# Cross-covariance attention into a folded MLP: block 2 of the fold ahead of the first tile, and w_in's first 512 columns loaded ahead of v

## The chip, the cores and the metric

The kernel runs on one core of a Trainium2 chip. The core has five engines with a queue each: TensorE (PE; its weight loads are shown as PEld), VectorE (DVE), ScalarE (ACT), GpSimd (POOL) and SyncE (SP). Sixteen DMA engines move data between memory and the on-chip buffer SBUF. PE writes its results to PSUM, which is divided into banks of 2 KB per partition. The metric is the time of one execution on the device in microseconds (us). A profile is one execution, with every instruction's start and duration; its times count from the first instruction.

## The reference

There are four batches of 6080 tokens, and 256 channels.

```python
qn = q / (np.linalg.norm(q, axis=1, keepdims=True) + 1e-06)   # norms over the 6080 tokens
kn = k / (np.linalg.norm(k, axis=1, keepdims=True) + 1e-06)
s = kn.transpose(0, 2, 1) @ qn / tau                          # 256 x 256 in each batch
a = softmax(s)                                                # over the last axis
x = (v @ a).reshape(24320, 256)
h = x @ w_in                                                  # w_in: 256 x 2048
g = s_moe * maximum(h, 0) ** 2 + b_moe
out = g @ w_out                                               # w_out: 2048 x 256
```

`tau` is 1.0. All inputs and the output are float32; the kernel works in float16 with float32 sums.

## The kernel before, in words

Attention and the first layer are folded into one matrix. With e the unnormalised exponentials, v @ a @ w_in = v @ (a @ w_in), and wa = a @ w_in is a 256 x 2048 matrix for each batch. So there is one product v @ wa for each tile of 512 tokens, then relu, the square, and the product with w_out. There are 48 tiles (the last is half a tile), and each takes 16 steps, one per slice of 128 hidden columns. `mm1(g, m)` (L744) makes slice m of tile g on PE: two products (one for each half of the 256 channels) of a 128x128 piece of `wa` with `vT`, the transposed tile of v. ACT then takes the relu of two slices at a time (L771), the squares are shared by DVE and ACT, and the second product follows later (L932, or L836 for the plain first tile).

Before the first tile, batch 0 has a prologue of its own. q and k are loaded in chunks through POOL's DMA queue, and cast to float16 on the way. PE sums the Gram matrix `s_ps` (L154). The norms come from squares, summed with ones on PE (`n_ps`, L252 and L256), and four ACT steps (L277) make their inverses. `scale` (L302, DVE) and `exps` (L308, ACT) make the exponentials `eT`, in two halves j = 0, 1. Batches 1 to 3 do the same later, spread out between the steps of the tiles.

Nothing reorders these instructions: `po` keeps every engine's instructions in the order in which the program is written. Semaphores between engines, and the choice of PSUM banks and buffers, are worked out when the kernel is built, from what each instruction reads and writes.

What touches the change:

- *Loads* (L524 to L539). POOL's queue gets, in this order: v's first tile, w_in's columns 0 to 255, 256 to 511, 512 to 1023, 1024 to 1535, 1536 to 2047, v's second tile, and four pieces of w_out. At most eight loads are under way; a load is issued when the one eight places before has landed.
- *The transposes* (`transpose_v(0)`, L594 and L463). Eight PE products with an identity turn v's first tile into `vT_ps`, one PSUM bank in float16. DVE copies it to `vT` in one instruction of 128x1024 (L471).
- *One idle matmul* (`keep_busy(1)`, L595 and L554). It has no use but to keep PE active.
- *The first block* (`first_block(2 * P)`, L340). For each half j of `eT`: two products for the row sums `r_ps` (L347), and two products with w_in's columns 0 to 255 (L352), for the two halves m of wa's rows. These lie in two banks. DVE takes the reciprocal of the sums (L356). Then `scaled` (L325) multiplies 128 columns at a time by it, into `wa`: m = 0 on ACT (L329), m = 1 on DVE (L331).
- *The other blocks* (`fold_one`, L361, listed at L430). Columns 256 to 511 (block 2), 512 to 767, 768 to 1023, 1024 to 1535 and 1536 to 2047, each in two halves m: two products each (L336) and a `scaled`. `FOLDS` (L667) puts them behind `mm1` of steps 0, 0, 1, 1, 3, 3, 5, 5, 8, 8 of the first tile. PE's order before is thus: transposes, idle matmul, first block, `mm1(0, 0)`, block 2, `mm1(0, 1)`, block at 512, `mm1(0, 2)`, and so on.
- *Banks.* Batch 0 takes its fold results from three banks in turn (`ps_o`, by `bank`, L442), `r_ps` among them. `s_ps` has a bank of its own.

Of the kernel before, what the change touches and what calls it, by code (L numbers as in the profile page):

```python
# [9 lines left out]
FP32 = mybir.dt.float32  # L10
# [6 lines left out]
def kernel(  # L17
# [12 lines left out]
    nc = tc.nc  # L30
    P = 128

    B, N, C = q.shape
# [11 lines left out]
    CH = C // P  # L45
# [9 lines left out]
    def po(ins):  # L55

        tc.keep_in_program_order(ins)
        return ins

    def pool(name, bufs, **kw):  # L60
        return ctx.enter_context(tc.tile_pool(name=name, bufs=bufs, **kw))
# [19 lines left out]
    ps_gram = pool("ps_gram", 1, space=PSUM)  # L81
# [4 lines left out]
    w_in16 = wpool.tile([P, CH, Dff], FP16)  # L86
# [4 lines left out]
    def h_tile(name):  # L91
        return ps_h.tile([P, 2, TG], FP32, tag="h_ps", name=name)
# [19 lines left out]
    class Gram:  # L112
# [147 lines left out]
        def finish_ops(self):  # L260

            st = {}

            def inverse(a=None):

                n = C + CH if a is None else (CH, C)[a]

                def part(i):
                    if i == 0:
                        st["r", a] = sm_pool.tile([P, n], FP32, tag=f"r{a}", name=f"r{a}")  # L270
                        if a is None:
                            st["r", 1], st["r", 0] = st["r", a][:, :C], st["r", a][:, C:]
                    r = st["r", a]
                    func, kw = [(AF.Ln, dict(bias=tiny)), (AF.Exp, dict(scale=0.5)),
                                (AF.Ln, dict(bias=eps)), (AF.Exp, dict(scale=-1.0))][i]
                    sums = self.n_all if a is None else self.n_ps[a]
                    po(nc.scalar.activation(out=r, in_=r if i else sums, func=func, **kw))  # L277
                    if i == 3 and a != 1 and inv_tau != 1.0:
                        po(nc.vector.tensor_scalar_mul(
                            out=st["r", 0], in0=st["r", 0], scalar1=inv_tau))  # L280

                return [lambda i=i: part(i) for i in range(4)]

            def norms(a):
                return lambda: self.add_norms(a, last=True)
# [9 lines left out]
            def scale(halves=1):  # L295
                rk, src = st["r", 1], st.get("t", self.s_ps)
                if "t" not in st:
                    st["t"] = sm_pool.tile([P, CH, C], FP32, tag="sm_t", name="sm_t")
                for h in range(halves):
                    js = slice(h, h + 1) if halves == CH else slice(0, CH)  # L300
                    n = js.stop - js.start
                    po(nc.vector.tensor_mul(st["t"][:, js], src[:, js],  # L302
                                            rk[:, None, :].broadcast_to((P, n, C))))

            def exps(j):
                if j == 0:
                    st["e"] = sm_pool.tile([P, CH, C], FP16, tag="eT", name="eT")
                po(nc.scalar.activation(  # L308
                    out=st["e"][:, j, :], in_=st["t"][:, j], func=AF.Exp,
                    scale=st["r", 0][:, j : j + 1]))  # L310
                if j == 0:
                    self.wa = apool.tile([P, CH, Dff], FP16, tag="wa16", name="wa16")
# [11 lines left out]

            def scaled(f0, n, m, wa_ps):  # L325
                dst = self.wa[:, m, ds(f0, n)]
                third = self.b == 0 and f0 == 2 * NW
                if m == third and not (self.b == 0 and NW <= f0 < 2 * NW):
                    po(nc.scalar.mul(out=dst, in_=wa_ps, mul=st["rs"][:, m : m + 1]))  # L329
                else:  # L330
                    po(nc.vector.tensor_scalar_mul(  # L331
                        out=dst, in0=wa_ps, scalar1=st["rs"][:, m : m + 1]))
# [4 lines left out]
                                        w_in16[:, j, ds(f0, n)],  # L337
                                        start=(j == 0), stop=(j == CH - 1)))

            def first_block(n):  # L340

                two = [self.bank("wa_ps", CH, C)[:, 0, :n], h_tile("wa_ps")[:, 0, :n]]
                r_ps = self.bank("r_ps", CH, C)[:, :, 0]
                for j in range(CH):
                    exps(j)
                    for ch in range(CH):
                        po(nc.tensor.matmul(r_ps[:, ch : ch + 1], st["e"][:, j, ts(ch, P)],  # L347
                                            parts16, start=(ch == 0 and j == 0),
                                            stop=(ch == CH - 1 and j == CH - 1),
                                            skip_group_check=True))  # L350
                    for m in range(CH):
                        po(nc.tensor.matmul(two[m], st["e"][:, j, ts(m, P)],  # L352
                                            w_in16[:, j, :n],
                                            start=(j == 0), stop=(j == CH - 1)))
                st["rs"] = sm_pool.tile([P, CH], FP32, tag="rs", name="rs")
                po(nc.vector.reciprocal(out=st["rs"], in_=r_ps))  # L356
                for f0 in range(0, n, P):
                    for m in range(CH):
                        scaled(f0, P, m, two[m][:, ds(f0, P)])

            def fold_one(f0, n, m):  # L361
                def f():
                    wa_ps = self.bank("wa_ps", CH, C).rearrange("p a c -> p (a c)")[:, :n]
                    fold_mm(f0, n, m, wa_ps)
                    if self.b == 0 and f0 == 2 * NW and m == 1:
                        return at_step(5, lambda: scaled(f0, n, m, wa_ps))
                    scaled(f0, n, m, wa_ps)
                return f
# [58 lines left out]
                ]  # L427

            if self.b == 0:
                blocks = [(2 * P, 2 * P), (4 * P, 2 * P), (6 * P, 2 * P), (2 * NW, NW), (3 * NW, NW)]  # L430
                folds = [fold_one(f0, n, m) for f0, n in blocks for m in range(CH)]
                return [norms(1), *inverse(1), norms(0), *inverse(0), lambda: scale(CH),
                        lambda: first_block(2 * P)] + folds

            def sums_and_halves():
                sums()
# [12 lines left out]
    def group(g):  # L449
        t0 = g * TG  # L450
        return t0, min(TG, NT - t0) // P

    v_tiles, vT_tiles = {}, {}

    def load_v(g):
        t0, nj = group(g)
        v16 = vpool.tile([P, TG // P, C], FP16, tag="v16", name="v16")
        po(nc.gpsimd.dma_start(  # L458
            out=v16[:, :nj, :],
            in_=v_flat[t0 : t0 + nj * P, :].rearrange("(p j) c -> p j c", j=nj)))  # L460
        v_tiles[g] = v16

    def transpose_v(g):  # L463
        _, nj = group(g)
        v16 = v_tiles.pop(g)
        vT_ps = ps_o.tile([P, CH, TG], FP16, tag="o_ps", name="vT_ps")
        for j in range(nj):
            for ch in range(CH):
                po(nc.tensor.transpose(vT_ps[:, ch, ts(j, P)], v16[:, j, ts(ch, P)], ident16))  # L469
        vT = vtpool.tile([P, CH, TG], FP16, tag="vT", name="vT")  # L470
        po(nc.vector.tensor_copy(out=vT[:, :, : nj * P], in_=vT_ps[:, :, : nj * P]))  # L471
        vT_tiles[g] = vT

    def crossbar_v(g):

# [31 lines left out]
    for c in range(NDIRECT, len(g0.chunks) - NLATE):  # L507
        g0.load(c)
        if c == NDIRECT:
            po(nc.gpsimd.affine_select(  # L510
                out=ident16, in_=ones_id, compare_op=ALU.is_equal, fill=0.0, base=0,
# [5 lines left out]
    NW = 512  # L517
    w_in_rows = moe_w_in.rearrange("(co p) f -> p co f", p=P)

    def load_w_in(f0, f1, co=None):  # L520
        cs = slice(0, CH) if co is None else slice(co, co + 1)
        po(nc.gpsimd.dma_start(out=w_in16[:, cs, f0:f1], in_=w_in_rows[:, cs, f0:f1]))

    load_v(0)  # L524
    load_w_in(0, 2 * P)
    load_w_in(2 * P, NW)
    load_w_in(NW, 2 * NW)
    load_w_in(2 * NW, 3 * NW)
    load_w_in(3 * NW, Dff)
# [21 lines left out]
    def keep_busy(n):  # L551

        for _ in range(n):
            po(nc.tensor.matmul(h_tile("idle_ps")[:, 0, :], fill[:, :P], fill, start=True,  # L554
                                stop=True, skip_group_check=True))

    norms_k, *rest = g0.finish_ops()
    inverse_k, norms_q, inverse_q, scale_s, first_block, folds = (
        rest[:4], rest[4], rest[5:9], rest[9], rest[10], rest[11:])
# [31 lines left out]
            g0.add_norms(0)  # L591
    for f in (*inverse_q, scale_s):
        f()
    transpose_v(0)  # L594
    keep_busy(1)  # L595
    first_block()


    acc = opool.tile([P, 4, C], FP32, tag="o_sb", name="acc")
# [64 lines left out]
    FIN = (0, 3, 5, 7, 9, 11, 13, 17, 19, 22,  # L664
           25, 27, 31, 33, 35, 37, 39, 41, 43, 47, 49, 51, 53, 55)
    first_group = [b * N // TG for b in range(B)]
    FOLDS = (0, 0, 1, 1, 3, 3, 5, 5, 8, 8)  # L667
    for i, f in enumerate(folds):
        early.setdefault(FOLDS[i], []).append(f)
    at_step(14, lambda: po(nc.vector.tensor_scalar_mul(  # L670
        out=s_out, in0=s_bc, scalar1=1.0 / (LAM * LAM))))
# [29 lines left out]
    for b in range(1, B):  # L701
# [6 lines left out]
        n = NCH * JC  # L708
# [247 lines left out]
    for s in range(NS + FT):  # L956
        g, m = divmod(s, FT)
# [8 lines left out]
        if work:  # L966
            items, n = work[0]
# [61 lines left out]
```

## Time and profile before

| What | us |
|---|---|
| median of 3 runs | 714.37 (714.33 to 714.67) |
| profiled execution: span, first to last instruction | 712.9 |
| profiled execution: its total | not on its page; the runs' median lies 1.5 above the span |
| PE busy, share of the span | 692.9 (97%) |
| DVE busy | 635.6 (89%) |
| ACT busy | 547.5 (77%) |
| first product of the first tile (L761) starts | 37.84 |
| PE idle just ahead of it | 0.48 |

In the lines shown below, a row of the chain has a start, a length, an engine and its work; a row of the timeline has a start, the time that the group took, the engine, line, operation, output and inputs, count and, in brackets, how long the engine was idle before and what ended that. In the table of stretches each engine has busy us and a count of instructions, followed by the granted TensorE clock (1.00 is full speed), the DMA engines' share and GB/s. The lines of the queues have packets, MB and the share of sixteen engines. The granted clock is the share of full speed at which PE was let run.

### The profile page before, as it was taken

How to read it: one execution, taken by the hardware profiler on the slowest of the kernel's cores; microseconds unless marked ns; L12 is line 12 of the kernel's file. 1: busy time of each engine (PE TensorE's matmuls, PEld its weight loads, DVE VectorE, ACT ScalarE, POOL GpSimd, SP SyncE). 2: the span in 40 equal slices, each digit the busy share in tenths (PEclk: the TensorE clock that was granted, in tenths of full speed). 3: DMA queues.
4: the chain of work that ended last, by engine and by line, in shares of the span. 5: the costliest groups of instructions: out<-in, count | busy, mean ns of one | idle time of the engine just before them, and what ended most of it. 6: DMA issues, size and time to landing. Idle time of an engine off the chain costs nothing.

```text
span 712.9 us, 17531 instructions
## 1 busy us (share of the span) xinstructions
PE 692.9 (97%) x7422; PEld 502.9 (71%) x7422; DVE 635.6 (89%) x906; ACT 547.5 (77%) x598; POOL 114.1 (16%) x192
## 2 busy tenths in 40 slices
PE   3699999999999999999999999999999999999998
PEld 2456777776677777777677777777768777777777
DVE  4889999999988989998999899998998888888886
ACT  5689877787777777778877777777876777777875
POOL 4533132201202222111010222111000000000000
PEclk9999999999999999999999999999999999999999
DMA  9999999566566878465761888737323333321202
GB/s 213 207 259 168 186 164 137 114 109 122 105 136 109 133 137 144 110 92 101 156 131 50 148 134 150 129 76 96 101 65 75 94 71 75 97 61 46 83 31 75
DMA packets 87854, 83.55 MB, mean 117 GB/s; under 512 B 56368, under 2 KB 62784, under 8 KB 87776
## 3 DMA queue, kind: packets, MB, share of 16 engines
q0 software_dynamic: 27136, 44.00, 38.9%
q1 hardware_dynamic: 60128, 37.45, 21.1%
q8 instruction: 58, 0.95, 0.6%
q10 hardware_dynamic: 512, 0.98, 0.4%
q14 instruction: 20, 0.16, 0.1%
HBM read 78.91 MB, written 24.90 MB: 146 GB/s over the span
## 4 chain that ended last, share of the span: by engine, by line
PE 95%; DMA 4%; ACT 1%; issue 0%; DVE 0%; ACTq 0%; POOLq 0%
PE h_ps L761 46%; PE o_ps L932 40%; PE s_ps L154 5%; DMA qk<-in_q_dram 2%; DMA qk<-in_k_dram 1%; PE wa_ps L394 1%; PE o_ps L836 1%; PE o_ps L808 0%; PE wa_ps L336 0%; ACT r L277 0%; PE n_ps L252 0%; ACT sq L185 0%; ACT eT L308 0%; PE vT_ps L469 0%; DVE half L229 0%
## 5 line engine op out<-in xcount | busy, mean ns | idle before, releaser
L771 ACT ACTIVATE r<-h_ps 128x1024 f16<-128x1024 f32 (+1 forms) x384 | 388.5, 1013 | 144.2 <-PE h_ps L761 140.6
L761 PE MATMUL h_ps<-vT,wa 128*128 128x512 f16 (+7 forms) x1632 | 452.1, 364 | 0.5 <-ACT wa L329 0.5
L932 PEld LDWEIGHTS <-S 128*128 128x128 f16 x2944 | 198.1, 98 | 84.3
L932 PEld LDWEIGHTS <-g 128*128 128x128 f16 x2208 | 155.0, 98 | 74.0
L784 DVE TENSOR_TENSOR g<-r 128x2048 f16<-128x2048 f16 (+2 forms) x150 | 174.4, 1163 | 10.1 <-ACT r L771 9.7
L932 PE MATMUL o_ps<-T,S 128*128 128x128 f16 x2208 | 183.1, 219 | 0.0
L761 PEld LDWEIGHTS <-wa 128*128 128x128 f16 x1632 | 136.6, 98 | 19.0 <-ACT wa L329 1.0
L932 PE MATMUL o_ps<-w_out,g 128*128 128x128 f16 x1472 | 134.2, 219 | 0.0
L782 ACT ACTIVATE g<-r 128x1024 f16<-128x1024 f16 (+1 forms) x97 | 100.3, 1034 | 0.2
L789 DVE SCALAR_TENSOR_TENSOR o_sb<-o_ps,s_out,u 128x256 f32<-128x256 f32 x138 | 66.2, 480 | 36.1 <-PE o_ps L932 34.5
L154 PE MATMUL s_ps<-qk 128*128 128x256 f16 (+1 forms) x384 | 71.0, 287 | 15.6 <-ACT qk L145 11.0
L458 POOL DMA_DIRECT2D v<-in_v_dram x48 | 31.4, 662 | 239.9 <-DMA vT<-v 192.7
L215 POOL DMA_DIRECT2D f<-f x33 | 28.8, 874 | 245.9 <-DVE f L199 197.3
L789 DVE SCALAR_TENSOR_TENSOR u<-o_ps,s_out,rowconst 128x256 f32<-128x256 f32 x138 | 65.7, 476 | 0.0
L932 PE MATMUL o_ps<-w_out,S 128*128 128x128 f16 x736 | 63.5, 219 | 0.0
L932 PE MATMUL o_ps<-N,g 128*128 128x128 f16 x736 | 63.4, 219 | 0.0
L185 ACT ACTIVATE sq<-qk 128x1024 f16<-128x1024 f16 (+2 forms) x53 | 54.5, 1041 | 4.5 <-DMA qk<-in_k_dram 1.9
L861 DVE TENSOR_TENSOR S<-S,g 128x2048 f16<-128x2048 f16 (+1 forms) x47 | 56.4, 1200 | 1.2
L859 DVE TENSOR_TENSOR S<-g 128x2048 f16<-128x2048 f16 (+1 forms) x47 | 56.0, 1192 | 0.0
L863 DVE TENSOR_TENSOR S<-g 128x2048 f16<-128x2048 f16 x46 | 55.8, 1214 | 0.0
L865 DVE TENSOR_TENSOR S<-g,S 128x2048 f16<-128x2048 f16 x46 | 55.8, 1213 | 0.0
L154 PEld LDWEIGHTS <-qk 128*128 128x128 f16 (+1 forms) x384 | 33.0, 103 | 21.2 <-ACT qk L145 11.0
(103 smaller groups left out, 334.4 us busy)
## 6 DMA issues: line engine op xcount, KB each, us to landing
out_dram<-o_sb SPq DMA_DIRECT2D x43, 512.0 KB, 3.0
v<-in_v_dram POOLq DMA_DIRECT2D x47, 256.0 KB, 5.0
qk<-in_q_dram POOLq DMA_DIRECT2D x43, 256.0 KB, 7.7
qk<-in_k_dram POOLq DMA_DIRECT2D x42, 256.0 KB, 6.4
f<-f POOLq DMA_DIRECT2D x30, 128.0 KB, 3.1
vT<-v SPq DMA_TRANSPOSE x182, 3.0
w<-in_moe_w_out_dram POOLq DMA_DIRECT2D x4, 512.0 KB, 9.9
out_dram<-o_sb SPq DMA_DIRECT2D x8, 256.0 KB, 4.1
```

Of the source, the lines that this page charges most:

```text
L154: po(nc.tensor.matmul(self.s_ps[:, ch, :], qc[:np_, j, ts(ch, P)], kc[:np_, j, :], start=(c == 0 and j == 0 and ch == 0), stop=(c == len(s ...
L185: po(nc.scalar.activation(out=st["sq"][:np_, a, js, :], in_=(qc, kc)[a][:np_, js, :], func=AF.Square))
L761: po(nc.tensor.matmul(dst, wa[:, ci, ts(m, P)], src, start=(ci == 0), stop=(ci == CH - 1), skip_group_check=True))
L771: po(nc.scalar.activation(out=r16[:, :, i % 2, :n], in_=h_tiles.pop((g, i))[:, :, :n], func=AF.Relu))
L782: po(nc.scalar.activation(out=dst, in_=src, func=AF.Square))
L784: po(nc.vector.tensor_mul(dst, src, src))
L789: po(nc.vector.scalar_tensor_tensor(out=dst, in0=src, scalar=s_out, op0=ALU.mult, in1=add, op1=ALU.add))
L859: po(nc.vector.tensor_add(T[1], A21, A22))
L861: po(nc.vector.tensor_sub(T[2], T[1], A11))
L863: po(nc.vector.tensor_sub(T[3], A11, A21))
L865: po(nc.vector.tensor_sub(T[4], A12, T[2]))
L932: po(nc.tensor.matmul(st[name][:, j, :], a()[:, i, ts(j, P)], w[:, i, :], start=first, stop=last, skip_group_check=True))
```

## The change

Three things change, all ahead of the first tile's second slice:

1. `first_block` also makes block 2: four products with w_in's columns 256 to 511, into one bank (`second`, both halves m side by side), right behind the first block's products. Its two `scaled` calls follow those of the first block. Block 2 leaves the list of later blocks and `FOLDS`. `r_ps` moves to the bank of `s_ps`. In both blocks `scaled` now has m = 0 on DVE and m = 1 on ACT.
2. `load_w_in` for columns 0 to 255 and 256 to 511 comes before `load_v(0)`.
3. `transpose_v(0, True)` copies `vT` in two halves of 128x512: the first on DVE, the second on ACT. ACT's half is written in the program behind the exponentials and block 2's products (`between`). The idle matmul is removed.

```diff
             def scaled(f0, n, m, wa_ps):
                 dst = self.wa[:, m, ds(f0, n)]
-                third = self.b == 0 and f0 == 2 * NW
+                third = self.b == 0 and (f0 == 2 * NW or f0 < NW)
...
-            def first_block(n):
+            def first_block(n, between):
 
                 two = [self.bank("wa_ps", CH, C)[:, 0, :n], h_tile("wa_ps")[:, 0, :n]]
-                r_ps = self.bank("r_ps", CH, C)[:, :, 0]
+                second = self.bank("wa_ps", CH, C)[:, :, :n]
+                r_ps = ps_gram.tile([P, CH, C], FP32, tag="s_ps", name="r_ps")[:, :, 0]
...
+                for m in range(CH):
+                    for j in range(CH):
+                        po(nc.tensor.matmul(second[:, m], st["e"][:, j, ts(m, P)],
+                                            w_in16[:, j, ds(n, n)], start=(m == 0 and j == 0),
+                                            stop=(j == CH - 1), skip_group_check=True))
+                between()
                 st["rs"] = sm_pool.tile([P, CH], FP32, tag="rs", name="rs")
...
+                for m in range(CH):
+                    scaled(n, n, m, second[:, m])
...
-                blocks = [(2 * P, 2 * P), (4 * P, 2 * P), (6 * P, 2 * P), (2 * NW, NW), (3 * NW, NW)]
+                blocks = [(4 * P, 2 * P), (6 * P, 2 * P), (2 * NW, NW), (3 * NW, NW)]
...
-    def transpose_v(g):
+    def transpose_v(g, split=False):
...
         vT = vtpool.tile([P, CH, TG], FP16, tag="vT", name="vT")
+        vT_tiles[g] = vT
+        if split:
+            po(nc.vector.tensor_copy(out=vT[:, 0], in_=vT_ps[:, 0]))
+            return lambda: po(nc.scalar.copy(out=vT[:, 1], in_=vT_ps[:, 1]))
         po(nc.vector.tensor_copy(out=vT[:, :, : nj * P], in_=vT_ps[:, :, : nj * P]))
-        vT_tiles[g] = vT
...
-    load_v(0)
     load_w_in(0, 2 * P)
     load_w_in(2 * P, NW)
+    load_v(0)
     load_w_in(NW, 2 * NW)
...
-    transpose_v(0)
-    keep_busy(1)
-    first_block()
+    first_block(transpose_v(0, True))
...
-    FOLDS = (0, 0, 1, 1, 3, 3, 5, 5, 8, 8)
+    FOLDS = (1, 1, 3, 3, 5, 5, 8, 8)
```

## The prediction

> **What bounds the kernel now.** I read the page's chain first: it says which engine's work sets the end.
>
> ```profile
> PE 95%; DMA 4%; ACT 1%; issue 0%; DVE 0%; ACTq 0%; POOLq 0%
> ```
>
> TensorE (PE) carries it. The chain in order of time says where PE has holes; from 37.84 us on it runs through PE alone, so whatever moves that start moves the end one for one:
>
> ```profile
> 35.95 0.52 ACT eT L308
> ...
> 36.96 0.17 PE r_ps L347 x2
> 37.13 0.02 issue
> 37.16 0.18 DVE rs L356
> ...
> 37.42 0.38 ACT wa L329
> 37.80 0.05 issue
> 37.84 0.60 PE h_ps L761 x2
> 38.45 0.44 PE wa_ps L336 x4
> ```
>
> The timeline of that stretch shows the hole that the change fills (0.48 us ahead of 37.84), and that v's transposes were already the last to be released, by v's DMA:
>
> ```profile
> 28.31 0.53 POOL L458 DMA_DIRECT2D v<-in_v_dram  x1 [0.80 <-DMA qk<-in_k_dram]
> 29.55 0.74 POOL L522 DMA_DIRECT2D w_in<-in_moe_w_in_dram  x1 [0.70 <-DMA qk<-in_q_dram]
> 30.75 2.13 POOL L522 DMA_DIRECT2D w_in<-in_moe_w_in_dram  x3 [0.47 <-DMA qk<-in_k_dram]
> ...
> 35.38 0.45 PEld L469 LDWEIGHTS <-v 128*128 128x128 f16 x8 [0.39 <-DMA v<-in_v_dram]
> 35.82 0.47 PE L554 MATMUL idle_ps<-fill 128*128 128x512 f32 x1
> 36.06 0.68 DVE L471 COPY vT<-vT_ps 128x1024 f16<-128x1024 f16 x1
> 37.84 0.60 PE L761 MATMUL h_ps<-vT,wa 128*128 128x512 f16 x2 [0.48 <-ACT wa L329]
> ```
>
> Last, the DMA view of 35.5 to 37.2 us, whose second line is a fetch of instructions among the loads, and the table of stretches (PE's busy us, then granted clock in the third column from the end):
>
> ```profile
> q0 software_dynamic: 442, 0.33, 128.0%
> q8 instruction: 1, 0.02, 3.6%
> ```
> ```profile
> 20.18:23.60 3.42, 1.66 (x12) 0.96 (x10) 3.28 (x7) 1.73 (x3) 1.06 (x3) 1.00 1.12 210
> 23.60:27.01 3.41, 1.53 (x12) 1.12 (x13) 3.17 (x8) 2.67 (x3) 1.58 (x4) 1.00 1.12 210
> 27.01:30.43 3.42, 3.39 (x16) 2.05 (x14) 2.16 (x5) 2.11 (x2) 1.77 (x3) 0.50 1.13 205
> ```
>
> **The base.** The profiled execution's span is 712.9 us; the page gives no total for it, and the runs' median of 714.37 lies 1.5 us above the span. I take that 1.5 as constant and add differences to 714.37. I measure at one point: PE's first fold product of the block at column 512, which before issues at 39.16 us (38.29 start of block 2's four products, 0.43; two products of the second slice, 0.44). Ahead of it both kernels have the same work in another order; behind it the order is the same.
>
> **Part 1: block 2's four products into the hole.** Four products of 256 columns leave the stretch after 37.84: 38.72 - 38.29 = 0.43 us off PE's dense part, if the hole stays where it was. The idle matmul (L554, 0.47 us) goes too; it lay in a wait for the exponentials (eT ends at 36.86), so it costs nothing by itself, but PE loses that activity. The sums r_ps move to the bank of s_ps, which the DVE has read by 36.14: nothing.
>
> **Part 2: two w_in loads past v on POOL's queue.** POOL issues w_in, w_in, v in the slots 28.31, 29.55 and 30.75. What these issues wait for (landings of q and k) is untouched; the later loads keep their places. The DMA engines are saturated there, so landing goes by place in the queue. From issue to landing the view gives v 7.0, w_in 6.4, 7.2 and 7.4 us: 35.31, 35.95, 37.95, 38.86. The three bring 256, 128 and 128 KB, together 512 KB in either order. Bounds for v in third place: by rate, 35.95 plus 128 KB at the stretch's 201 GB/s, 0.65: **36.6**; by the record of third place, **37.95**. The difference is the fetch q8, one 16 KB packet in this stretch, on one of 16 engines; the landing counts all 16. The second w_in load, in third place, had it; nothing waited for it, for its products came at 38.29. Would v have it? The page has 58 such packets on q8 against 14,844 PE instructions, one in 256, so the position in PE's program triggers them; up to the transposes that program is unchanged, and this fetch should come at the same time. The third place is then hit whoever stands in it. Against it: v's issue takes 0.53 us, not 0.71, and the fetch could fall just behind v. I take 37.95, as the row of the same place, and keep 36.6 as the other end.
>
> **Part 3: who waits for v.** In the built order of the changed kernel the eight transposes still stand ahead of the sums and fold products on PE. Those needed only eT and w_in; now they queue behind v. Call T the first transpose, 0.07 after landing (35.31 to 35.38). All from rows of before:
> - transposes to copy: 36.06 - 35.38 = 0.68. The DVE's half copy: 1024 elements take 0.68, f16 sums of 512 take 0.42; I take 0.42, so T+1.10.
> - ACT's half. In the built order it waits for a DVE instruction, not for PE; the nearest one that fits is the DVE's half. So the halves run in series. ACT's 128x512 scaling takes 0.68, with consecutive starts about 0.1 closer: start T+1.17, next instruction at T+1.76. No row shows such a pair side by side; if it were, 0.2 less.
> - ACT's first scaling 0.37 and 0.04 to PE: T+2.17. The DVE meanwhile does the reciprocal (0.17) and its scaling (0.37), T+1.7, so the product's first half starts earlier; the second starts at T+2.17.
> - three products of 0.216 to the measuring point: **T+2.82**.
>
> The PE work before that (0.43 transposes, about 0.55 first block, 0.43 second) ends near T+1.6 and hides in it. ACT's copy is new work (0.65), in front of the scalings that PE waits for; the DVE's saving (0.27) is off the path.
>
> *A rule.* The order above has ACT wait for the DVE on a tile that both only read. The Trainium skill, "PSUM — Partial Sum Buffer", section "PSUM bank collisions raise a hardware error", says that two engines must be kept apart on one bank, reads against reads included. vT_ps is one bank, so by it the sharing is a serial hand-over; with the 0.2 us of an overlap the end would be 0.2 earlier. No run here shows a collision.
>
> Sum, at full clock: T = 38.02 gives 40.84, **+1.68 us**; T = 36.67 gives 39.49, **+0.33**.
>
> **Part 4: PE's clock.** The last Gram product ends at 35.28. With T = 38.02 PE is idle for 2.74 us. The table has a stretch of 3.41 us with PE busy for 1.53 and half clock in the next one, and one with 1.66 that is followed by full clock. The stretch 33.84 to 37.25, where PE was busy for 3.08, would have 35.28 - 33.84 = 1.44. So I expect half clock from 37.25 to 40.67. At half clock 40 Gram products took 7.37 us, 0.184 each, against 0.11 at full: 0.073 more per 256 columns. Transposes, first and second block are four such each: 0.3 each. Transposes delay the copies by 0.3; PE's own chain now reaches its first product at T+2.5, behind ACT no more; with one slow product the measuring point is near T+3.4, 41.4: **+2.3**. Bounds: nothing, if the clock stays; half of 3.41, 1.7 more, if the slow stretch falls on dense work.
>
> *A rule.* The skill, "TensorE: Matmul & The Clock Gate", section "Why this matters for your kernels", asks for no idle gaps above some 3 us. The gap of 2.74 is under that; by the rule the clock stays and the sum is +1.68. This trace halves the clock after a stretch without any gap above 1.3 us, so I go by the row.
>
> The forecast is 714.37 + 2.3 = **716.7**.
>
> **Rivals.**
> 1. *v is not hit by the fetch* and lands at 36.6: T = 36.67, PE idle for 1.4 us, the stretch to 37.25 busy for 2.0, above 1.66, so full clock: 714.7, not slower by what can be told. This is the rival on the other side; it decides if v lands before about 37.7 (39.16 + 1.43 - 2.82 - 0.07). For it: the short issue of v. Against it: the landing record of third place.
> 2. *The clock holds* with v late: 716.05. For it: the half clock is seen once. Against it: 1.44 lies below 1.53.
> 3. *The gain of part 1 comes through*: the hole filled and v not late, 713.9. It needs T + 2.82 at 38.73, so v by 35.84. But q's last load lands at 34.0 (27.00 + 7.0), and 512 KB at 201 GB/s take 2.6 us from there. Not even this is 0.2% faster.
> 4. *The slow stretch falls on dense work*, or lasts for two stretches: 717.8 to 718.3.
>
> **How the numbers follow.** 0.2% is 1.43 us, about what a measurement of this kernel can tell from no change. Chances: forecast 0.38; rival 1 0.38; rival 2 0.12; rival 4 0.08; rival 3 or something unseen 0.04. Same: rival 1 and part of rival 2 that ends under 715.8, 0.42; slower 0.55; faster 0.03. The range takes rival 1's lower half (714.5) to between the prices of rival 4 (718.0); above 715.8 alone it would be 715.9 to 718.0.
>
> **What would show it.** v's issue at 30.75 and its landing near 37.95 (or 36.6); the first transpose released by that DMA; the sums and fold products right behind the transposes, eT long done; ACT's half copy starting after the DVE's end; a wait of PE on ACT's scaling at T+2; a clock of 0.50 in a stretch near 37 to 41; from the block at column 512 on, the timeline of before shifted as a whole. Wrong if the fetch moves, if the transposes do not hold back the sums, or if PE's later order has slack that absorbs the shift.

## The result, and the profile after

The changed kernel takes 717.3 us (median of 7 executions) against 714.45 for the kernel before (7 executions): ratio 1.0035, 95% interval 1.0024 to 1.0046. It is slower by about 2.9 us, more than the 0.2% that can be told from no change.

The single times say more than the median. The kernel before lies between 714.3 and 715.5. The changed kernel gave 714.77, 716.06, 717.15, 717.30, 717.31, 718.27 and 718.38, and the one execution that was profiled is the quickest of them (span 713.1 us, 1.7 around it). That profile cannot show the loss. I had the same kernel run once more, which gave a profiled execution of 717.48 us (span 715.8). I call the two profiles *after* and *again*.

The page's chain is the first view, of *after*, and it reads as before: PE carries the kernel.

```profile
PE 94%; DMA 5%; issue 0%; DVE 0%; DVEq 0%; POOLq 0%
```

The chain in order of time, of *after*:

```profile
30.76 5.86 DMA v<-in_v_dram
36.62 0.05 issue
36.67 0.64 PE vT_ps L478 x8
37.30 0.02 issue
37.33 0.42 DVE vT L482
37.75 0.09 DVE rs L363
37.94 0.36 DVE wa L331
38.31 0.05 issue
38.35 1.17 PE h_ps L771 x4
39.52 0.44 PE wa_ps L336 x4
```

Before, the chain here ran through the exponentials and ACT's scaling. Now it starts at v's load: issue at 30.76, landing at 36.62. The same view of *again*:

```profile
30.69 7.39 DMA v<-in_v_dram
38.07 0.05 issue
38.12 0.62 PE vT_ps L478 x8
...
39.22 0.45 PE wa_ps L353 x2
39.67 0.85 PE wa_ps L358 x4
40.52 1.71 PE h_ps L771 x4
42.23 0.44 PE wa_ps L336 x4
```

Here v lands 1.45 us later, and four products (`h_ps`, L771) take 1.71 us where four at full clock take 0.86 (the next four in the same view). The tables of stretches say why. PE's busy time stands right behind the stretch's length, the granted clock third from the end. *After*:

```profile
35.59:39.00 3.41, 2.24 (x23) 1.58 (x24) 2.02 (x7) 2.32 (x7) 2.17 (x4) 1.00 1.22 200
39.00:42.42 3.42, 3.42 (x22) 1.94 (x21) 2.78 (x7) 2.69 (x4) 1.48 (x3) 1.00 1.13 294
```

*Again*:

```profile
35.27:38.69 3.42, 0.57 (x11) 0.57 (x12) 0.76 (x2) 1.42 (x5) 1.55 (x4) 1.00 1.21 200
38.69:42.10 3.41, 3.41 (x18) 1.83 (x16) 1.78 (x5) 1.59 (x4) 2.19 (x4) 0.50 1.15 266
```

With v on time PE is busy for 2.24 us of the stretch and the clock stays at 1.00. With v late it is busy for 0.57 us, and the next 3.41 us run at 0.50. PE has plenty to do in that second stretch (3.41 of 3.41 busy), so half clock is time lost.

The same in the timeline. First *after*, where the whole hand-over can be read:

```profile
36.67 0.62 PE L478 MATMUL vT_ps<-ident,v 128*128 128x128 f16 x8 [1.38 <-DMA v<-in_v_dram]
37.33 0.42 DVE L482 COPY vT<-vT_ps 128x512 f16<-128x512 f16 x1 [1.18 <-PE vT_ps L478]
37.79 0.58 ACT L483 COPY vT<-vT_ps 128x512 f16<-128x512 f16 x1 [0.92 <-DVE vT L482]
38.35 1.17 PE L771 MATMUL h_ps<-vT,wa 128*128 128x512 f16 x4
38.69 0.35 PEld L771 LDWEIGHTS <-wa 128*128 128x128 f16 x3 [0.25 <-ACT wa L329]
39.35 0.60 PE L336 MATMUL wa_ps<-w_in,eT 128*128 128x256 f16 x4
```

Then *again*:

```profile
38.12 0.62 PE L478 MATMUL vT_ps<-ident,v 128*128 128x128 f16 x8 [2.91 <-DMA v<-in_v_dram]
40.32 1.91 PE L771 MATMUL h_ps<-vT,wa 128*128 128x512 f16 x4
42.02 0.65 PE L336 MATMUL wa_ps<-w_in,eT 128*128 128x256 f16 x4
```

The last line of each is the measuring point of the prediction, PE's first fold product of the block at column 512: 39.16 before, 39.35 in *after*, 42.02 in *again*. The spans are longer by 0.2 and by 2.9 us. Whatever moves that point moves the end one for one, as the prediction assumed.

The 2.86 us of *again* split in three. The first transpose T moves from 36.67 to 38.12: 1.45. From T to the point, *after* needs 2.68 and *again* 3.90: 1.22 for the clock. The rest, 0.19, is what *after* itself loses.

### The profile page after: what moved, and what is told of

It reads as the page before. It is cut to its first block, busy times and chain, and to the rows that moved or that the text cites. A ratio compares the mean times of both kernels' runs of the same rounds, so it can differ in the third digit from the quotient of the medians.

```text
span 713.1 us, 17531 instructions
## 1 busy us (share of the span) xinstructions
PE 691.6 (97%) x7421; PEld 502.1 (70%) x7421; DVE 635.3 (89%) x906; ACT 547.9 (77%) x599; POOL 113.9 (16%) x192
## 3 DMA queue, kind: packets, MB, share of 16 engines
q1 hardware_dynamic: 60128, 37.45, 22.0%
## 4 chain that ended last, share of the span: by engine, by line
PE 94%; DMA 5%; issue 0%; DVE 0%; DVEq 0%; POOLq 0%
PE h_ps L771 46%; PE o_ps L942 40%; PE s_ps L154 5%; DMA qk<-in_q_dram 2%; DMA qk<-in_k_dram 1%; PE wa_ps L403 1%; PE o_ps L846 1%; DMA v<-in_v_dram 1%; PE o_ps L818 0%; PE wa_ps L336 0%; PE vT_ps L478 0%; PE rc_ps L620 0%; DVE vT L482 0%; DVE wa L331 0%; DVE o_sb L824 0%
## 5 line engine op out<-in xcount | busy, mean ns | idle before, releaser
L771 PE MATMUL h_ps<-vT,wa 128*128 128x512 f16 (+7 forms) x1632 | 452.3, 365 | 0.1
L771 PEld LDWEIGHTS <-wa 128*128 128x128 f16 x1632 | 136.6, 98 | 18.9 <-DVE wa L331 0.6
L799 DVE SCALAR_TENSOR_TENSOR o_sb<-o_ps,s_out,u 128x256 f32<-128x256 f32 x138 | 66.5, 482 | 36.0 <-PE o_ps L942 34.2
L154 PEld LDWEIGHTS <-qk 128*128 128x128 f16 (+1 forms) x384 | 32.5, 102 | 21.3 <-ACT qk L145 11.1
```

Of the source, the lines that this page charges most:

```text
L154: po(nc.tensor.matmul(self.s_ps[:, ch, :], qc[:np_, j, ts(ch, P)], kc[:np_, j, :], start=(c == 0 and j == 0 and ch == 0), stop=(c == len(s ...
L771: po(nc.tensor.matmul(dst, wa[:, ci, ts(m, P)], src, start=(ci == 0), stop=(ci == CH - 1), skip_group_check=True))
L799: po(nc.vector.scalar_tensor_tensor(out=dst, in0=src, scalar=s_out, op0=ALU.mult, in1=add, op1=ALU.add))
```

## The experiments

Nine runs followed, the first of them of the changed kernel again. "Before" in each comparison is the kernel before on the same chip: 714.42, 714.43 and 714.35 us (medians of 21, 32 and 15 executions in the three groups). Four questions: which part of the change costs the time, what the clock's share is, why the third load lands late, and what the rest of the change is worth once nothing is late.

### 1. The changed kernel again

No edit.

> The changed kernel once more, for more executions and a second trace: the profiled execution of 714.77 us is one of the fast end, while the median is 717.3. Late v with a slower clock (the forecast): most executions between 716 and 718.4; a trace of one of them has v's load landing near 37.9, not 36.6, and one or two stretches of half clock more than the fast one. Clock alone (rival): v lands at 36.6 in every trace, and a slow execution differs from a fast one only by stretches of half clock behind 35 us.

Measured: 717.2 us (715.88, 717.09, 717.20, 717.48, 717.90), ratio 1.0038 [1.0025, 1.0050]. The profile is the one read above. Of the twelve executions of this kernel one took 714.8, two about 716, and nine 717.1 to 718.4 us. The mean granted clock of an execution goes with this: 0.998 in the three quickest, 0.992 to 0.997 in the other nine. What differs from *after* to *again* is v's landing, 36.62 and 38.07, and then the clock.

### 2. v first, the rest of the change kept

```diff
+    load_v(0)
     load_w_in(0, 2 * P)
     load_w_in(2 * P, NW)
-    load_v(0)
     load_w_in(NW, 2 * NW)
```

> The changed kernel with the loads in the order of before (v, then w_in's two pieces); block 2's products stay ahead of the first tile and the copy stays shared. If the loss is v's place in the queue: the first transpose is back at 35.38, PE is never idle for long, so the executions agree within 0.5 us. With the second w_in piece landing at 36.6 the point of measurement (the first product of the block at column 512) is near 38.7 to 38.8, 0.4 us ahead of before: 714.0. With that piece landing at 37.9 block 2's products wait for it in front of the first tile: the point near 39.3, 714.6. If the loss came from the shared copy or from block 2's place: still 716 or more.

Measured: 714.45 us (11 executions, ten from 714.15 to 714.61 and one of 715.91), ratio 1.0000 [0.9991, 1.0009]. The loss is gone with the order of the loads alone; the filled hole, the shared copy and the missing idle matmul cost nothing that can be measured. They also gain nothing, and the timeline says why:

```profile
37.60 0.60 PE L358 MATMUL wa_ps<-w_in,eT 128*128 128x256 f16 x4 [0.56 <-DMA w_in<-in_moe_w_in_dram]
38.04 1.03 PE L771 MATMUL h_ps<-vT,wa 128*128 128x512 f16 x4
```

Block 2's products now wait 0.56 us for the second w_in load, which is in third place again and lands late in v's stead (37.56).

### 3. The order of the loads alone

In the kernel before, with nothing else changed:

```diff
-    load_v(0)
     load_w_in(0, 2 * P)
     load_w_in(2 * P, NW)
+    load_v(0)
     load_w_in(NW, 2 * NW)
```

> The kernel before with the order of the three loads alone changed. v's place in the queue as the cause: with v at 36.6 the transposes start at 36.67, the one copy ends at 38.03, the first product starts near 38.7, and the point of measurement, behind 0.43 + 0.43 + 0.43 us of products, is near 40.0: 715.2; with v at 37.9 it is 1.3 us more, 716.5; half clock adds up to 1.7 to either, so the median lies at 716 to 718, and the executions spread by 2 us or more. The changed copy and the place of block 2 as the cause: 714.4, as before.

Measured: 717.67 us (717.51 to 717.92, 5 executions), ratio 1.0046 [1.0033, 1.0059]. One moved line gives all of the loss, and slightly more. The timeline and the table of stretches show the same two steps:

```profile
37.77 0.62 PE L469 MATMUL vT_ps<-ident,v 128*128 128x128 f16 x8 [2.79 <-DMA v<-in_v_dram]
39.78 1.04 PE L761 MATMUL h_ps<-vT,wa 128*128 128x512 f16 x2 [0.28 <-ACT wa L329]
```
```profile
35.35:38.76 3.41, 0.99 (x13) 0.84 (x14) 0.82 (x3) 1.14 (x4) 1.66 (x3) 1.00 1.21 199
38.76:42.17 3.41, 3.13 (x14) 1.49 (x13) 1.60 (x5) 1.10 (x3) 1.92 (x4) 0.50 1.14 289
```

### 4. PE kept busy while it waits for v

In the changed kernel, five idle matmuls ahead of the transposes:

```diff
+    keep_busy(5)
     first_block(transpose_v(0, True))
```

> The changed kernel with five idle matmuls between the last Gram product and the transposes, in time in which PE waits for v anyway (5 x 0.24 us = 1.2 of at least 1.35). If half clock after PE's idle stretch makes the executions above 716.1: these go, and what is left is v's landing alone, 714.8 with v at 36.6 and 716.1 with v at 37.9. If the clock plays no part: the same spread as the changed kernel's, median 717.3.

Measured: 715.78 us (11 executions), ratio 1.0018 [1.0009, 1.0027]. v is late as before (T = 37.49 in this execution), but the stretch that was nearly empty is now busy for 2.09 us, and no half clock follows:

```profile
34.10:37.51 3.41, 2.09 (x19) 1.29 (x18) 0.76 (x2) 2.17 (x7) 2.25 (x3) 1.00 1.22 206
37.51:40.92 3.41, 3.33 (x30) 2.27 (x31) 1.92 (x6) 2.05 (x5) 1.85 (x3) 1.00 1.20 218
```
```profile
34.58 1.60 PE L566 MATMUL idle_ps<-fill 128*128 128x512 f32 x5
37.49 0.62 PE L478 MATMUL vT_ps<-ident,v 128*128 128x128 f16 x8 [1.32 <-DMA v<-in_v_dram]
40.18 0.60 PE L336 MATMUL wa_ps<-w_in,eT 128*128 128x256 f16 x4
```

T to the measuring point is 2.69, as in *after*. So the late landing by itself costs 1.36 us in the times, and the clock about as much again (717.2 - 715.78 = 1.4 between medians; 1.22 in the profile).

### 5. The fetch of instructions pushed back

The theory was that a fetch of PE instructions (queue q8) delays whichever load stands third. The trace's landing records have an entry for each of the 16 parts of a load. For the third load, in us:

```
kernel         third load   15th part   16th part   fetch on q8 starts
before         w_in         36.61       37.91       35.89
v_first        w_in         36.27       37.56       35.45
loads_alone    v            36.29       37.72       35.70
again          v            36.55       38.07       36.05
busy           v            36.15       37.45       35.33
after          v            36.52       36.62       35.83
```

In five of the six profiles fifteen parts land within a normal time, and one part 1.3 to 1.5 us later. In *after* the sixteenth lands only 0.10 behind the fifteenth. The fetch itself takes 0.97 us on one of the 16 DMA engines. To test it I shortened PE's program ahead of that point by 32 instructions, leaving out two chunks of the Gram products:

```diff
         # Gram.mm
+            if self.b == 0 and c in (1, 2):
+                return
```

> The changed kernel without 16 of batch 0's Gram products (chunks 1 and 2, all four rows each), which leaves that part of the sum out. They lie in the first 20 us, in which PE waits for loads, so they cost no time; but PE's program is 32 instructions shorter ahead of the place that triggers the instruction fetch. If the place in PE's program sets the fetch, and the fetch holds up one of the sixteen parts of v's load: the fetch starts after 37 us instead of at 35.3 to 36.1, v's last part lands with the other fifteen, at 36.6, in every execution, the first transpose is 0.7 us behind the exponentials' end or less, and the time is 714.3 to 715.0 with a spread below 1 us. If the fetch keeps its time, or v is held up by something else: 716 to 718 as before.

Measured: 714.48 us (714.25 to 714.86, 11 executions), ratio 1.0001 [0.9992, 1.0009]. All of the loss is gone although the load order is that of the changed kernel, and so is the spread between executions: the eleven lie within 0.6 us. v's sixteen parts land by 36.23, and only the *fourth* load still has a straggler (fifteenth part 37.52, sixteenth 38.64), which nobody waits for here. All the profiles have one there, 0.65 to 1.15 us behind; in *after* it is 38.56 against 37.91:

```profile
36.28 0.62 PE L480 MATMUL vT_ps<-ident,v 128*128 128x128 f16 x8 [1.38 <-DMA v<-in_v_dram]
37.96 1.17 PE L773 MATMUL h_ps<-vT,wa 128*128 128x512 f16 x4
38.96 0.60 PE L338 MATMUL wa_ps<-w_in,eT 128*128 128x256 f16 x4
```

One thing was not as expected: I had put the fetch after 37 us, and it starts at 36.06, at a time at which it hurts *again* (36.05). So the time counted from the first instruction does not decide. Counted from the fetch's start to the landing of the third load's fifteenth part, the five profiles with a straggler have 0.50 to 0.82 us and this one 0.13; in experiments 7 to 9, whose third load has at most a small one, it is -0.12, -0.01 and 0.22. *After*, with 0.69, is the exception. What fits these rows is the fetch's place in the order of its own engine, ahead of the last packets of the third load or behind them. The packets in the trace do not name their engine, so this finer point is a reading. That moving the fetch takes the loss away is shown.

Leaving the products out did not by itself make the rest earlier: the last Gram products start at 34.30 here, and at 34.22 to 34.69 in the six profiles of the table. The first tile's first product and the measuring point lie at the same distance from T as in *after* (1.68, 2.68).

### 6. The fetch pulled forward

Eight more idle matmuls (16 PE instructions) among the Gram products:

```diff
-    FILL = {-8: 1, -7: 1, -6: 1, -5: 2, -4: 2}
+    FILL = {-9: 1, -8: 3, -7: 3, -6: 2, -5: 4, -4: 2}
```

> The changed kernel with eight more idle matmuls in the prologue, in gaps in which PE waits for loads: 16 instructions more ahead of the fetch. If the place in PE's program sets it: the fetch starts some 2.5 us earlier, near 33.4; one part of q's last load is late by 1.0 (34.9 instead of 34.0), the end of the Gram products moves by as much, v lands near 37.9, and no execution is below 715.7. If time or the loads set it: the fetch stays near 35.9, and so does everything else.

Measured: 715.67 us (9 executions, six of them from 715.45 to 715.73, the others 716.77, 716.90 and 718.04), ratio 1.0024 [1.0015, 1.0034]. The fetch moved forward, to 32.94; the DMA view of 32.5 to 34.2 us has it, where before has no such line:

```profile
q0 software_dynamic: 508, 0.32, 128.8%
q8 instruction: 1, 0.02, 3.6%
```

But it did not get out of the way. It now stands ahead of q's last load, too: issued at 27.0 in both kernels, that load takes 8.1 us to land, 7.0 before. DVE's squares wait for it, and PE waits 0.92 us for the squares ahead of the last Gram products (timeline):

```profile
35.22 0.42 DVE L182 TENSOR_TENSOR sq<-qk 96x512 f16<-96x512 f16 x1 [1.15 <-DMA qk<-in_q_dram]
35.69 0.25 PE L256 MATMUL n_ps<-ones,sq 96*128 96x1 f16 x4 [0.92 <-DVE sq L182]
35.81 0.60 PE L154 MATMUL s_ps<-qk 96*128 96x256 f16 x4
37.49 0.62 PE L478 MATMUL vT_ps<-ident,v 128*128 128x128 f16 x8 [1.09 <-DMA v<-in_v_dram]
40.18 0.60 PE L336 MATMUL wa_ps<-w_in,eT 128*128 128x256 f16 x4
```

The Gram products of the third line started at 34.68 before. v is late all the same, though by less than I had expected (37.9): its fifteenth part lands at 36.66, its sixteenth at 37.45. So the delay of one part is not made up by the third load. Five of the nine executions lie just below the 715.7 that I had named as the least. The measuring point, T + 2.69, is 1.02 later than before; the times say 1.24. The clock stays at 1.00: PE is busy for 2.28 us from 33.20 to 36.62, as the Gram products come late, too. So the earlier fetch delayed more loads; of the two places tried, only the later one helped.

### 7. The fetch back and v first

Experiments 5 and 2 together: v and w_in's second piece are not hit, and the hole is filled.

> The same omission of 16 Gram products, with the loads in the order of before (v, then w_in's two pieces); block 2 stays ahead of the first tile. If the fetch was what kept block 2's products waiting (0.56 us of PE's time on w_in's second piece): that piece lands with the others, PE goes from the first block's products to block 2's without a wait, and the time is 0.4 us under before: 714.0. If the hole cannot be filled for another reason, the time stays at 714.4.

Measured: 714.28 us (11 executions), a few tenths above what I had expected, ratio 0.9997 [0.9988, 1.0006]. This is the gain that the change could have had. Since the prologue shifts by some tenths between executions, I measure from the start of the exponentials (36.01 here, 35.95 before) to the measuring point: 2.95 us against 3.21, so 0.26 us or 0.04%, in one profile of each; the times alone cannot tell it from nothing.

```profile
37.25 0.60 PE L360 MATMUL wa_ps<-w_in,eT 128*128 128x256 f16 x4
37.89 1.05 PE L773 MATMUL h_ps<-vT,wa 128*128 128x512 f16 x4
38.96 0.33 PEld L338 LDWEIGHTS <-eT 128*128 128x128 f16 x4 [0.51 <-DMA w_in<-in_moe_w_in_dram]
38.96 0.61 PE L338 MATMUL wa_ps<-w_in,eT 128*128 128x256 f16 x4
```

Block 2's products stand in the former hole (37.25), without a wait for w_in's second piece. Of the 0.43 us of those products 0.26 show. The rest is lost at the measuring point itself: its weight load waits for w_in's next piece, the fourth load, whose straggler lands at 38.92. The first tile's four products, 0.22 us apart, would have let it start at 38.78, so the wait costs 0.18. (The hole of about 0.2 us that stays ahead of 37.89, in which PE waits for the scaling, is not the reason: the first tile's first product comes 1.88 us behind the start of the exponentials, 1.89 before.) Experiment 9 confirms it: there no product waits for a load, and the exponentials' start lies 2.78 us ahead of the measuring point (36.34, 39.12), 0.43 less than before.

### 8. The copy of v whole, on DVE alone

Experiment 5 with the copy undivided:

```diff
-    first_block(transpose_v(0, True))
+    transpose_v(0)
+    first_block(lambda: None)
```

> The same omission of 16 Gram products, changed kernel's load order, but the copy of vT whole on the DVE. The shared copy runs in series (in the trace ACT's half starts 0.04 us after the DVE's end), yet the first tile's first product needs the DVE's half only. By the rows: whole copy 0.68 after the transposes, reciprocal 0.17, scaling 0.37: the first product 2.0 us behind the first transpose, against 1.68 in the changed kernel. So 0.2 to 0.3 us more than with the shared copy. If sharing is worth nothing, the two are equal.

Measured: 714.86 us (11 executions), ratio 1.0007 [0.9999, 1.0016], against 714.48 for the shared copy. In the profile T to the first product takes 1.95 us whole and 1.68 shared, and T to the measuring point 2.84 and 2.68. Sharing is worth 0.16 us by one profile of each kernel and 0.4 by the medians, whose intervals overlap.

### 9. A complete kernel with v first and fewer idle matmuls

The change with v first, and five idle matmuls fewer, which shortens PE's program by 10 instructions without leaving work out:

```diff
-    FILL = {-8: 1, -7: 1, -6: 1, -5: 2, -4: 2}
+    FILL = {-5: 1, -4: 1}
```

> A complete kernel: loads in the order of before, block 2 ahead of the first tile, shared copy, and five of the prologue's seven idle matmuls left out, eight instructions of them ahead of the fetch. If eight are enough to put the fetch behind w_in's second piece: that piece lands at 36.6, block 2's products run without a wait, and the time is that of the run with the omitted Gram products, 714.3, 0.1 to 0.2 us under before. If they are not enough: 714.45 as with all idle matmuls. If the missing activity slows PE's clock behind 33 us: up to 1.7 us more.

Measured: 714.56 us (11 executions, 714.15 to 716.50) against 714.35, ratio 1.0005 [0.9996, 1.0014]. The straggler is nearly gone (the last two parts of w_in's second piece land at 36.34 and 36.73, and PE does not wait for them), but in this profile the clock is halved for two stretches among the Gram products, which then end about 0.3 us later. The mean clock is 0.995 or less in all eleven executions, and in one of 15 before, so fewer idle matmuls did cost clock:

```profile
26.00:32.83 6.83, 5.27 (x22) 3.33 (x23) 5.42 (x12) 4.41 (x5) 4.12 (x7) 0.50 1.15 206
```

The exponentials start at 36.34, 0.39 later than before, and that spends the 0.43 gained behind them. No complete kernel that was run beats the kernel before by an amount that can be measured.

## Why the prediction was right, point by point

The direction was right, and the measured 717.3 lies in the range, 0.6 us above the predicted 716.7.

**Part 1, the hole.** Priced at 0.43 us off PE's dense part. Where no product waits for a load it is 0.43 (experiment 9, from the exponentials' start to the measuring point), and 0.26 where the fourth load's straggler takes 0.18 of it (experiment 7). The price was right; in the changed kernel it is buried under v's wait.

**Part 2, v in third place.** I took the landing of that place before, 37.95, and kept 36.6 as the other end. Both happen: 38.07 in *again* (37.72 and 37.45 in two other kernels), 36.62 in *after*. The reason named, the instruction fetch on one of the 16 engines, is shown by experiment 5: moved, it takes the loss with it. I had treated the two values as two answers of which one is true. They are two outcomes of one kernel; what makes an execution go one way or the other is not shown. The forecast and rival 1 had the same chance, and nothing in the prediction settled which would be the usual one, so that part is luck. The kernel before carries the same straggler, in a load that nobody waits for.

**Part 3, who waits for v.** T to the measuring point was put at 2.82 and is 2.68 in *after* and 2.69 in experiment 4. ACT's half does start after DVE's half, 0.04 us behind its end, so the serial hand-over is right; it takes 0.58 and not 0.65, which is half of the difference. PE's wait for ACT's scaling, forecast at T+2, is there as well: 0.25 us of its weight loads, up to 38.69, T+2.02. The rule that I weighed there (the Trainium skill, "PSUM — Partial Sum Buffer", section "PSUM bank collisions raise a hardware error") speaks of engines kept apart on one bank; the runs agree in that the two reads never overlap, and none shows what a collision would do.

Parts 2 and 3 gave +1.68 at full clock, against 1.64 in the rows (T of *again*, 38.12, and the 2.68 of *after*) and 1.36 in the times of experiment 4.

**Part 4, the clock. This is the term that was mis-sized.** I had the half clock from 37.25 to 40.67 and its price at about 0.6 us (from +1.68 to +2.3), because that stretch would have ended at T+2.65, with one of the first tile's products slow. It came from 38.69 to 42.10 in *again* and from 38.76 to 42.17 in experiment 3, over dense work; it ended at T+3.98 in *again*, with all four products slow (1.71 us, not 0.86), and cost 1.22 us. The price of slow work was low, too: the 0.184 us for 256 columns came from 40 Gram products between 10.96 and 18.33, and no row gives half clock there (the table of stretches has 1.00, and the trace's record of the clock begins only at 16.80). In *again* block 2's four products took 0.85, 0.21 each. The length, 3.41 us, was right; the place was not. I had carried the stretch boundaries over from the trace of before (33.84, 37.25), but the boundaries move from one execution to the next: half clock early in the prologue starts at 27.04 before, 21.94 in *after*, 21.62 in *again*. The prediction named the bounds over this phase, 0 to 1.7 us, but took a point between them as if the phase were known; a late v, I would argue now, makes the upper part likelier. The forecast's mechanism with rival 4's clock is what the usual execution shows: 2.86 us in *again*.

The activity that I read off the table, 1.53 us busy before a halved stretch and 1.66 before an unhalved one, pointed the right way. In the ten profiles whose trace records changes of the clock, cut at the recorded boundaries, it was halved after stretches in which PE was busy for 0.57, 0.99, 1.28, 1.37, 1.48, 1.54, 1.56 and 1.58 us, and kept after one of 1.52 and all of 1.59 and more. So by these rows the bound is near 1.55 of 3.41 us, not quite sharp in the trace's modelled busy times. The other rule that I weighed, the Trainium skill, "TensorE: Matmul & The Clock Gate", section "Why this matters for your kernels", asks for no gaps above some 3 us; the clock was halved after gaps of 2.91 (*again*) and 2.79 us (experiment 3), and after the six busier of these stretches, none of which has a gap above 1.5. Going by the row rather than by the rule was right here.

**The rivals.** Rival 1 (v at 36.6, 714.7) had the same chance as the forecast; its execution exists, *after* at 714.77, but only as one of twelve. Rival 2 (the clock holds, 716.05) is what experiment 4 makes at 715.78; the two executions of the changed kernel at about 716 fit it, with a mean clock of 0.998 as in *after*, but no trace of them shows it. Rival 3, a gain, never came. Rival 4 (717.8 to 718.3) fits the three slowest executions, but what sets them apart is not seen. Their mean clock, 0.992 and 0.993, speaks for a halved stretch more than *again* has (each takes 0.0024 off the mean: 3.41 us at half clock in 716), yet two executions at 717.1 and 717.2 have 0.993, too.

What stays open is why *after* escaped the fetch at 35.83 and *again* did not at 36.05, and so why one execution in twelve, and not half of them, goes the good way.

## What to carry to other kernels

Before moving a load into another place of a full queue, look at when that *place* lands, not at when the load landed: something else, here a 16 KB fetch of instructions on one of 16 DMA engines, may delay the place whoever stands in it, and PE starts on a load only when its last part has landed (38.07 and 38.12 in *again*). A wait of 1.4 us on an engine whose clock depends on its activity can cost twice that, so price the clock as a range over where the slow stretch may fall. When one profile of a changed kernel looks harmless and the median does not, profile it again before explaining anything.

## What was not expected of the hardware

- A kernel's program length ahead of a point shifts data transfers. 16 PE instructions more moved a fetch from about 35.9 to 32.94 us, where it delayed q's last load as well; with 32 fewer no part of v was held up, and the time was 2.8 us less. The Trainium skill, "Runtime: NRT & Kernel Launch", section "Instruction fetch mechanics", has the instruction buffer refilled in 16 KiB blocks of 256 instructions by a DMA queue of its own, at a cost that is "mostly hidden". The blocks agree (58 packets on q8 for 14,842 PE instructions). For PE itself the cost agrees: no row shown here has it waiting for instructions. But the fetch is not hidden from the loads: one fetch among saturated loads held back one part of a load by 1.3 to 1.5 us.
- The same kernel can be off by 3.6 us between executions (714.8 to 718.4); between its two profiles 1.45 us of the difference is the landing of one part of one load, and 1.22 the slow stretch behind it. With the fetch moved back, eleven executions lie within 0.6 us (1.2 with the undivided copy).
- Stretches at half clock are 3.41 us long, or twice that (6.83 in experiments 4 and 9), with a phase that differs from execution to execution.
